# Attention with a mixture of experts on one core: where the third value product of each group stands, and where the group's output is read

## The chip, the core and the metric

The kernel runs on one core of a Trainium2 chip. Its time is device microseconds for one execution. A core has TensorE (PE in the rows, its weight loads PEld), VectorE (DVE), ScalarE (ACT), GpSimd (POOL) and SyncE (SP), which issues most of the DMAs. Each engine works through its own list of instructions in order and waits at semaphores for the others. PSUM is the memory that TensorE writes to, in banks of 2 KiB per partition.

## The reference

Attention over 4 batches of 8 heads (576 positions, 64 columns), where scores more than `tau` below their row's maximum are dropped, then a mixture of 8 experts with one expert for each token, then a dense pair of layers. The case is about the attention part alone:

```python
scores = scale * np.matmul(q, k.transpose(0, 1, 3, 2))
thresh = np.max(scores, axis=-1, keepdims=True) - tau
scores = np.where(scores >= thresh, scores, -1000000000.0)
scores = scores - np.max(scores, axis=-1, keepdims=True)
attn = np.exp(scores)
attn = attn / (np.sum(attn, axis=-1, keepdims=True) + 1e-09)
return np.matmul(attn, v).astype(np.float32)
```

## The kernel before

Attention runs as 16 units. A unit is one head of two batches, 2 times 576 rows, cut into nine tiles of 128 rows; tile 4 holds the last 64 rows of both batches. Tile `t` of unit `u` is step 9u + t, so there are 144 steps, and units are counted from 0. `Attn.run` (L325) writes the order out by hand. In step `i` every engine's list gets: the jobs of phase 0; the scores of step i + 2 (`scores`, L198, TensorE); the jobs of phase 1; row maximum and exponential of step i + 1 (`smax` L221 on VectorE, `sexp` L227 on ScalarE); mask and row sum of step i (`smask`, L240, VectorE); the threshold of step i + 1 (L231, VectorE); then the jobs of phases 2 and 3. A score tile has one of three PSUM buffers from its scores to its mask.

The jobs come from the table `PL` (L305): `"po0": (14, 2)` says that a unit's first read of outputs goes to 14 steps after the unit's first step, phase 2. `PFIRST` and `PLAST` replace entries for the first and the last unit. Within a phase, jobs stand in the order of the units.

After the mask, `split_e` (L248, ScalarE) casts a tile to 16 bits and `split_l` (L252 and L253, GpSimd) takes the remainder. When three tiles, a group, are there, `tr_e` (L259) has a DMA transpose it, issued by SP. SP also issues the swap of the halves of the queries (L195), the loads of queries, keys and values (L90 to L105), and the stores of the attention output (L300, L301). `e16`, the transpose's source, has three buffers, and `et`, its result, four.

The value products (`pv`, L282, TensorE) follow 11 steps after the tile: 14 matmuls for a tile, 28 for tile 4, each with its weights load. They write the tile `ops`, one half of it for one group and the other half for the next. `ops` shares its PSUM bank with two smaller things: the logits of the router (`lm`, which `lg_add`, L545 or L543, reads on VectorE) and a sum over the values (`vsum`, read at L132). `pv_out` (L288, VectorE; jobs `po0`, `po1`, `po2`) reads a group's half, multiplies by the reciprocals and writes `x`.

Other jobs in the places that follow: the transposes of a later unit's queries and keys on TensorE (`tr`, L164, into the one tile `tps`; the jobs `q0` and `k5` are those that the change meets) and their evacuation on ScalarE (L186, L190); the largest absolute value of the values (L123), the row sums' reciprocals (L267, L268) and the scaling of the values (L137), all on VectorE; `lg_tr` (L528) and `lg_mm` (L536) of the router on TensorE.

In steps counted from a unit's first one, its products stand at 11 to 19, always in phase 3, so the third, sixth and ninth at 13, 16 and 19. The reads stand at 14 (phase 2) and, two of them together, at 20 (phase 3), just ahead of the next unit's first product.

Of the kernel before, what the change touches and what calls it, by code (L numbers as in the profile page):

```python
# [30 lines left out]
class Attn:  # L31
# [259 lines left out]
    def store(self, u):  # L291
        nc = self.nc
        P, h = divmod(u, H)
        if h % 2 == 1:
            c = slice((h - 1) * D, (h + 1) * D)
            X = self.X[u // 2]
            for j in range(2):
# [7 lines left out]
    PL = {"lq": (-21, 1), "lk": (-31, 2), "lv": (-12, 1), "hi0": (-16, 2), "hi1": (-15, 3), "lo0": (-13, 1),  # L305
# [6 lines left out]

    PFIRST = {"hi0": (-20, 2), "hi1": (-18, 0), "lo0": (-18, 0), "lo1": (-18, 1), "q0": (-17, 0), "eq0": (-16, 2),
# [3 lines left out]
    PLAST = {"te": (4, 3), "po0": (14, 1), "po1": (17, 0), "po2": (20, 0), "rc": (11, 1), "t0": (14, 2),  # L317
             "v0": (16, 3), "l0": (20, 2), "t1": (19, 3), "v1": (20, 3), "l1": (21, 0), "t2": (20, 3), "v2": (21, 3),
             "l2": (21, 3), "la": (24, 3)}

    AFTER = ["lq hi0", "lk hi1", "hi0 lo0", "hi1 lo1", "lo0 q0", "lo0 q4", "lo0 m", "lo1 m", "lo1 k0", "lo1 k5", "q0 eq0",
             "eq0 m", "m em", "em q4", "q4 eq4", "eq4 k0", "k0 ek0", "ek0 k5", "k5 ek5", "eq0 swap", "em swap", "eq4 swap", "vm vn", "vn vc", "vc vw", "vw vh", "vh vl", "se sl", "sl te", "po2 st",
# [2 lines left out]
    def run(self, units, moe=None):  # L325
        nc = self.nc
        NU = len(units)
        sched = {}
        PL = self.PL
        for x in self.AFTER:  # L330
            x, y = x.split()
            assert PL[x] < PL[y] or PL[x] == PL[y] and list(PL).index(x) < list(PL).index(y), (x, y)

        def at(b, job, f, *a):
            i, ph = PL[job]
            sched.setdefault((b + i, ph), []).append((f, a))

        for n, u in enumerate(units):
            b = 9 * n
            PL = {**self.PL, **(self.PFIRST if n == 0 else self.PLAST if n == NU - 1 else {})}  # L340
            if n % 4 == 0:
                e0 = 0 if n else 1
                at(b, "lq", self.load_qk, u // 4, 0, e0, 4)
                at(b, "lk", self.load_qk, u // 4, 1, e0, 4)
                at(b, "lv", self.load_v, u // 4)
                for e in range(4):
                    at(b + e, "vm", self.v_max, u + e)
                at(b, "vn", self.v_sum, u)
                at(b, "vc", self.v_scale, u)
            for i in range(2):  # L350
                at(b, f"hi{i}", self.split_hi, u, i)
            for i in range(2):
                at(b, f"lo{i}", self.split_lo, u, i)
            for w in ("q0", "m", "q4", "k0", "k5"):
                at(b, w, self.tr, u, w)
                at(b, "e" + w, self.evac, u, w)
            if n == 0:
                at(b, "swap0", self.swap, u, 0, 256)
            at(b, "swap", self.swap, u, 256 if n == 0 else 0)
            at(b, "vw", self.v_w, u)  # L360
            at(b, "vh", self.v_hi, u)
            at(b, "vl", self.v_lo, u)
            for t in range(9):
                at(b + t, "se", self.split_e, u, t)
                if n == NU - 1:
                    at(b + t, "se", self.split_l, u, t // 3, slice(t % 3, t % 3 + 1), nc.vector if t in self.LD else nc.gpsimd)
                elif t % 3:
                    at(b + t, "sl", self.split_l, u, t // 3, slice(2 * (t % 3 - 1), t % 3 + 1), nc.gpsimd)
                if t % 3 == 2:
                    at(b + t - 2, "te", self.tr_e, u, t // 3)  # L370
                at(b + t, "pv", self.pv, u, t)
            for g in range(3):
                at(b, f"po{g}", self.pv_out, u, g)
            at(b, "rc", self.recip, u)
            at(b, "st", self.store, u)
            if moe and u % 2 == 1:
                P, j = u // H, u % H // 2
                for g in range(3):
                    at(b, f"t{g}", moe.lg_tr, P, j, g)
                    at(b, f"v{g}", moe.lg_ev, P, j, g)  # L380
                    at(b, f"l{g}", moe.lg_mm, P, j, g)
                at(b, "la", moe.lg_add, P, j)
        steps = [(u, t) for u in units for t in range(9)]
        ps, nn, ee = {}, {}, {}
        first, last = min(sched)[0], max(sched)[0]
        for i in range(first, last + 1):
            if i == 4 and moe:
                moe.consts()
            for f, a in sched.get((i, 0), []):
                f(*a)  # L390
            if 0 <= i + 2 < len(steps):
                ps[i + 2] = self.scores(*steps[i + 2])
            for f, a in sched.get((i, 1), []):
                f(*a)
            if 0 <= i + 1 < len(steps):
                nn[i + 1] = self.smax(ps[i + 1])
                ee[i + 1] = self.sexp(ps[i + 1], nn[i + 1])
            if 0 <= i < len(steps):
                self.smask(*steps[i], ps.pop(i), nn.pop(i), ee.pop(i))
            if 0 <= i + 1 < len(steps):  # L400
                self.sthr(nn[i + 1])
            for ph in (2, 3):
                for f, a in sched.get((i, ph), []):
                    f(*a)
# [911 lines left out]
```

## Time and profile before

| | us |
|---|---|
| median of three runs | 1117.97 (1114.81 to 1119.68) |
| the profiled execution | 1115.51 |
| its span, first to last instruction | 1113.7 |
| TensorE busy in the span | 954.5 (86%) |
| VectorE busy | 904.8 (81%) |
| ScalarE busy | 655.0 (59%) |
| GpSimd busy | 725.6 (65%) |
| value products (L282), TensorE | 101.3 |
| reads of the outputs (L288), VectorE | 15.4 in 48 |

The span is 1.8 us shorter than the execution's time. Attention fills about the first third of it, up to some 370 us; the change touches nothing behind that. In the timeline a row gives the start and the length of a piece, the engine, the line, the operation with what it writes and reads, how many were merged, and in brackets how long the engine had been idle before it and what ended that. The busy shares of the whole span are a mean over stages with different limits, so the rows below come from stretches of the attention stage.

### The profile page before, as it was taken

How to read it: one execution, taken by the hardware profiler on the slowest of the kernel's cores; microseconds unless marked ns; L12 is line 12 of the kernel's file. 1: busy time of each engine (PE TensorE's matmuls, PEld its weight loads, DVE VectorE, ACT ScalarE, POOL GpSimd, SP SyncE). 2: the span in 40 equal slices, each digit the busy share in tenths (PEclk: the TensorE clock that was granted, in tenths of full speed). 3: DMA queues.
4: the chain of work that ended last, by engine and by line, in shares of the span. 5: the costliest groups of instructions: out<-in, count | busy, mean ns of one | idle time of the engine just before them, and what ended most of it. 6: DMA issues, size and time to landing. Idle time of an engine off the chain costs nothing.

```text
span 1113.7 us, 20722 instructions
## 1 busy us (share of the span) xinstructions
PE 954.5 (86%) x7297; PEld 879.9 (79%) x7297; DVE 904.8 (81%) x1628; ACT 655.0 (59%) x1223; POOL 725.6 (65%) x629
## 2 busy tenths in 40 slices
PE   4587776885977477999999999799999999999997
PEld 3476666774876377989999999688999999999986
DVE  4898877976978559885979875799989989898894
ACT  5687875875977134443445546576665656656652
POOL 3886875775878045554565657587776767667673
PEclk9688886887889678999999999899999999999999
DMA  7999999999999666686777876320100101000000
GB/s 177 170 203 192 213 200 195 217 185 208 180 187 190 143 227 229 216 280 216 251 246 278 283 259 200 112 79 15 43 22 19 46 11 41 15 29 1 20 10 29
DMA packets 249768, 162.51 MB, mean 146 GB/s; under 512 B 180122, under 2 KB 222508, under 8 KB 249661
## 3 DMA queue, kind: packets, MB, share of 16 engines
q1 hardware_dynamic: 245901, 150.36, 56.4%
q0 software_dynamic: 3312, 10.49, 2.7%
q8 instruction: 59, 0.97, 0.3%
q10 hardware_dynamic: 448, 0.30, 0.1%
q14 instruction: 48, 0.39, 0.1%
HBM read 85.08 MB, written 23.60 MB: 98 GB/s over the span
## 4 chain that ended last, share of the span: by engine, by line
PE 45%; DVE 13%; issue 3%; ACT 2%; DMA 2%; POOL 0%; POOLq 0%; DVEq 0%; SPq 0%; ACTq 0%
PE h L1008 22%; PE y L1082 15%; PE y L1063 7%; DVE w L1195 2%; DVE w L1196 2%; DVE cv L1116 2%; DVE cm L1114 1%; DVE w L1193 1%; DVE w L978 1%; DVE cm L1118 1%; PE t L985 1%; DVE tm L1194 1%; DMA xr<-rows,idx 1%; DVE w L1197 1%; DVE hbuf L1044 1%
## 5 line engine op out<-in xcount | busy, mean ns | idle before, releaser
L252 POOL TENSOR_TENSOR e<-em,e 128x1024 f16<-128x1024 f32 (+1 forms) x98 | 158.1, 1613 | 83.8 <-ACT e L248 50.5
L1192 POOL TENSOR_SCALAR tm<-u 128x384 uint8<-128x384 f32 x88 | 128.6, 1462 | 57.5 <-ACT u L1188 56.9
L1008 PE MATMUL h<-xa,w 128*128 128x256 f32 (+6 forms) x864 | 141.6, 314 | 5.7 <-DVE hbuf L1044 4.7
L1063 PE MATMUL y<-hbuf,w 128*128 128x256 f32 (+6 forms) x864 | 141.3, 312 | 5.8 <-DVE yo L1066 5.6
L227 ACT ACTIVATE e<-sps,n 128x576 f32<-128x576 f32 x144 | 108.0, 750 | 52.4 <-DVE n L221 51.9
L1008 PEld LDWEIGHTS h<-xa,w 128*128 128x128 f32 x864 | 131.4, 195 | 8.0 <-DVE hbuf L1044 5.8
L1063 PEld LDWEIGHTS y<-hbuf,w 128*128 128x128 f32 x864 | 128.2, 192 | 7.5 <-DVE yo L1066 6.6
L978 POOL TENSOR_TENSOR w<-raw,w 128x1024 fp32r<-128x1024 f32 x36 | 91.4, 2538 | 63.5 <-ACT w L976 31.4
L240 DVE SCALAR_TENSOR_TENSOR em<-sps,n,e 128x576 f32<-128x576 f32 x144 | 116.5, 809 | 17.8 <-ACT e L227 14.8
L282 PE MATMUL ops<-vh,et 128*128 128x64 f16 (+1 forms) x2240 | 101.3, 205 | 34.0 <-DVE x L288 30.6
L221 DVE TENSOR_REDUCE n<-sps 128x1 f32<-128x576 f32 x144 | 107.2, 744 | 24.5 <-PE sps L213 24.4
L282 PEld LDWEIGHTS <-et 128*128 128x128 f16 (+1 forms) x2240 | 88.9, 110 | 45.2 <-issue 36.3
L1195 DVE SCALAR_TENSOR_TENSOR w<-y,w 128x384 f32<-128x384 f32 x96 | 122.4, 1275 | 0.0
L1188 ACT ACTIVATE u<-h 128x384 f32<-128x384 f32 x96 | 47.1, 491 | 127.0 <-PE h L1008 126.8
L213 PE MATMUL sps<-ka,qa 128*128 128x288 f32 x320 | 90.2, 376 | 28.4 <-DVE em L240 22.3
L248 ACT CAST e<-em 128x576 f16<-128x576 f32 x144 | 97.2, 676 | 22.2 <-DMA et<-e 21.0
L1008 PE MATMUL h<-xk,w 128*128 128x384 f32 x576 | 109.6, 338 | 0.7 <-DVE w L978 0.5
L1209 POOL TENSOR_TENSOR gl<-w,gh 128x384 fp32r<-128x384 f32 x83 | 84.7, 1021 | 38.8 <-ACT gh L1208 38.8
L1008 PEld LDWEIGHTS h<-xk,w 128*128 128x128 f32 x576 | 102.7, 189 | 5.2 <-DVE w L978 0.8
L1043 ACT ACTIVATE hbuf<-h 128x256 fp32r<-128x256 f32 (+6 forms) x72 | 31.1, 431 | 127.2 <-PE h L1008 127.1
L1082 PE MATMUL y<-w,gh 128*128 128x512 f32 x258 | 82.1, 399 | 6.9 <-DVE yo L1066 6.9
L976 ACT CAST w<-raw 128x1024 fp32r<-128x1024 f32 x72 | 75.3, 1050 | 19.3 <-DVE poff L576 14.7
(224 smaller groups left out, 2261.1 us busy)
## 6 DMA issues: line engine op xcount, KB each, us to landing
raw<-in_moe_w_dram SPq DMA_DIRECT2D x64, 512.0 KB, 5.2
qb<-qa SPq DMA_DIRECT2D x30, 304.0 KB, 4.8
cv<-in_moe_w_in_dram SPq DMA_DIRECT2D x16, 512.0 KB, 5.1
cv<-in_moe_w_out_dram SPq DMA_DIRECT2D x16, 512.0 KB, 4.9
wscr<-cm SPq DMA_DIRECT2D x32, 256.0 KB, 2.5
raw<-wscr SPq DMA_DIRECT2D x16, 512.0 KB, 4.0
xw<-yT SPq DMA_DIRECT2D x24, 192.0 KB, 2.4
vv<-in_v_dram SPq DMA_DIRECT2D x8, 512.0 KB, 5.7
```

What stands on the lines that cost most here:

```text
L221: nc.vector.tensor_reduce(out=n[:, 0:1], in_=ps[:, :, 0:288], axis=AX.XY, op=ALU.max, negate=True)
L227: nc.scalar.activation(out=e, in_=ps[:, :, 0:288], func=AF.Exp, bias=n[:, 0:1])
L240: nc.vector.scalar_tensor_tensor(out=self.em[u, g][:, i].rearrange("p (a b) -> p a b", a=2), in0=ps[:, :, 0:288], scalar=n[:, 1:2], in1=e, ...
L248: self.nc.scalar.copy(self.e16[u, g][:, i, 0:S], self.em[u, g][:, i])
L252: eng.tensor_tensor(out=e16[:, r, S + 64:], in0=em[:, r, 0:512], in1=e16[:, r, 0:512], op=ALU.subtract)
L282: nc.tensor.matmul(o[q], lhsT=et[:, base + c, q], rhs=vh[:, a, j, c if c < 5 else c - 5, :], start=(n == 0), stop=(n == len(terms) - 1))
L978: (self.nc.gpsimd if pool else self.nc.vector).tensor_tensor(out=l, in0=raw, in1=h.bitcast(F32), op=ALU.subtract)
L1008: self.nc.tensor.matmul(out, lhsT=a, rhs=b, start=(i == 0), stop=(i == len(parts) - 1))
L1063: nc.tensor.matmul(self.ys[d], lhsT=a[:, f % 2, s], rhs=b, start=(f == 0 and i == 0), stop=(f == 7 and i == 2))
L1082: nc.tensor.matmul(self.ys[m], lhsT=a[:, s], rhs=b[:, f % 2], start=(f == 0 and i == 0), stop=(f == 15 and i == 2))
L1192: nc.gpsimd.tensor_scalar(out=mk, in0=u, scalar1=RCUT * RCUT, scalar2=None, op0=ALU.is_gt)
L1195: V.scalar_tensor_tensor(out=w, in0=y, scalar=b, in1=w, op0=ALU.add, op1=ALU.mult)
```

## The change

The table's one entry for the value products becomes nine, one for each tile. A group's first two products stay in phase 3; its third (tiles 2, 5 and 8) moves to phase 1 of the same step, that is right behind the scores of step i + 2. The group's read moves to phase 0 of the step that follows, so it is VectorE's first instruction there: `po0` from 14 phase 2 to 14 phase 0, `po1` from 20 phase 3 to 17 phase 0, `po2` from 20 phase 3 to 20 phase 0. The last unit keeps its order. No instruction is added or removed.

```diff
-          "se": (1, 2), "sl": (2, 0), "te": (4, 2), "pv": (11, 3), "po0": (14, 2),
-          "po1": (20, 3), "po2": (20, 3), "rc": (13, 1), "st": (32, 3), "t0": (23, 1), "v0": (24, 1), "l0": (31, 2),
+          "se": (1, 2), "sl": (2, 0), "te": (4, 2), "po0": (14, 0),
+          "po1": (17, 0), "po2": (20, 0), "rc": (13, 1), "st": (32, 3), "t0": (23, 1), "v0": (24, 1), "l0": (31, 2),
...
+    for t in range(9):
+        PL[f"pv{t}"] = 11 + t, 1 if t % 3 == 2 else 3
...
+    PLAST.update({f"pv{t}": (11 + t, 3) for t in range(9)})
...
-                at(b + t, "pv", self.pv, u, t)
+                at(b, f"pv{t}", self.pv, u, t)
```

On VectorE, at the fourteenth step of a unit (here one where the values of a later head are being reduced, L123), the difference of the two orders is this. L221, L240 and L231 are row maximum, mask and threshold.

```order
 L137 TENSOR_SCALAR vv<-vv,sc 128x2x320
 L123 TENSOR_REDUCE pm<-vv 128x1
-L221 TENSOR_REDUCE n<-sps 128x1
-L240 SCALAR_TENSOR_TENSOR em,su<-sps,n,e 128x576
-L231 TENSOR_SCALAR n<-n,ntau 128x1
-L288 TENSOR_TENSOR x<-ops,r 128x3x64
+L288 TENSOR_TENSOR x<-ops,r 128x3x64
+L221 TENSOR_REDUCE n<-sps 128x1
+L240 SCALAR_TENSOR_TENSOR em,su<-sps,n,e 128x576
+L231 TENSOR_SCALAR n<-n,ntau 128x1
 L123 TENSOR_REDUCE pm<-vv 128x1
```

The first group's read goes from the end of the step to its front, ahead of the maximum and the mask.

On VectorE, at the fourteenth step of a unit where the router's logits are added, before:

```order
L137 TENSOR_SCALAR vv<-vv,sc 128x2x320
L221 TENSOR_REDUCE n<-sps 128x1
L240 SCALAR_TENSOR_TENSOR em,su<-sps,n,e 128x576
L231 TENSOR_SCALAR n<-n,ntau 128x1
L545 TENSOR_TENSOR L<-L,ops 128x8x9
L288 TENSOR_TENSOR x<-ops,r 128x3x64
L221 TENSOR_REDUCE n<-sps 128x1
```

The same place now (four lines were added to the file, so L545 has become L549):

```order
L137 TENSOR_SCALAR vv<-vv,sc 128x2x320
L288 TENSOR_TENSOR x<-ops,r 128x3x64
L221 TENSOR_REDUCE n<-sps 128x1
L240 SCALAR_TENSOR_TENSOR em,su<-sps,n,e 128x576
L231 TENSOR_SCALAR n<-n,ntau 128x1
L549 TENSOR_TENSOR L<-L,ops 128x8x9
L221 TENSOR_REDUCE n<-sps 128x1
```

The read has gone to the front, and the addition of the logits, which reads the same bank, still ends the step.

On TensorE, at the sixteenth step of a unit, before: scores, then the four transposes of a later unit's queries, then the first of the sixth product's 14 matmuls.

```order
L213 MATMUL sps<-ka,qa_108 128x288 x2
L213 MATMUL sps<-ka,qb_110 128x288 x2
L164 MATMUL tps<-identr,x_2576 128x128 x4
L282 LDWEIGHTS et
L282 MATMUL ops<-vh,et 128x64
```

The same place now, from the last of those 14 matmuls on, which follow the scores directly:

```order
L282 LDWEIGHTS et
L282 MATMUL ops<-vh,et 128x64
L164 MATMUL tps<-identr,x_2578 128x128 x4
L213 MATMUL sps<-ka,qa_108 128x288 x2
L213 MATMUL sps<-ka,qb_110 128x288 x2
```

The sixth product has passed the transposes, which now stand directly ahead of the next scores. At the thirteenth step the third product passes the transposes of `k5` in the same way; at the nineteenth there are none to pass.

## Rows read from the trace of the kernel before

**Rows 1.** Waits, whole span: who waited for whom, us in total, times, longest.

```profile
PE ops L282 <- DVE x L288: 30.6, 24, 3.0
...
DVE n L221 <- PE sps L213: 24.4, 29, 3.7
...
ACT e L248 <- DMA et<-e: 21.0, 9, 4.2
...
DVE pm L123 <- DMA vv<-in_v_dram: 11.4, 3, 4.9
```

**Rows 2.** Sums of a stretch: length, busy us of each engine, granted clock, DMA.

```profile
core 0: us, PE busy (x) PEld busy (x) DVE busy (x) ACT busy (x) POOL busy (x), PEclk, DMA share, GB/s
104.40:193.60 89.20, 64.53 (x831) 59.23 (x831) 71.79 (x176) 64.50 (x114) 64.21 (x61) 0.81 1.08 206
```

**Rows 3.** Timeline of SP, 104.3 to 193: first and last of 29 pieces.

```profile
104.49 4.12 SPq L259 DMA_TRANSPOSE et<-e  x1
...
180.77 11.48 SPq L259 DMA_TRANSPOSE et<-e  x2
```

**Rows 4.** Timeline of SP: pieces around its idle places.

```profile
57.57 1.34 SPq L90 DMA_DIRECT2D raw<-in_q_dram  x2
61.51 6.04 SPq L259 DMA_TRANSPOSE et<-e  x1
...
99.04 4.72 SPq L259 DMA_TRANSPOSE et<-e  x1
...
193.69 4.03 SPq L259 DMA_TRANSPOSE et<-e  x1
198.35 1.10 SPq L195 DMA_DIRECT2D qb<-qa  x2
200.20 5.96 SPq L259 DMA_TRANSPOSE et<-e  x1
...
277.98 4.13 SPq L259 DMA_TRANSPOSE et<-e  x1
284.08 4.67 SPq L259 DMA_TRANSPOSE et<-e  x1
```

**Rows 5.** Timeline of step 68, 186 to 194: from maximum to subtraction.

```profile
186.12 0.74 DVE L221 TENSOR_REDUCE n<-sps 128x1 f32<-128x576 f32 x1
186.78 0.80 DVE L240 SCALAR_TENSOR_TENSOR em<-sps,n,e 128x576 f32<-128x576 f32 x1
186.96 0.74 ACT L227 ACTIVATE e<-sps,n 128x576 f32<-128x576 f32 x1 [2.06 <-DVE n L221]
...
187.64 0.34 DVE L288 TENSOR_TENSOR x<-ops,r 128x192 f32<-128x192 f32 x1
...
188.04 0.91 PE L282 MATMUL ops<-vh,et 128*128 128x64 f16 x14 [2.19 <-DVE x L288]
...
188.39 2.14 POOL L252 TENSOR_TENSOR e<-em,e 128x1024 f16<-128x1024 f32 x1 [3.27 <-ACT e L248]
...
193.35 0.32 POOL L253 TENSOR_TENSOR e<-em,e 128x64 f16<-128x64 f32 x1
```

**Rows 6.** Timeline of steps 70 and 71, 191.5 to 195: transposes, maximum, product.

```profile
193.53 0.67 PE L164 MATMUL tps<-identr,x 128*128 128x128 f32 x4
193.77 0.76 DVE L221 TENSOR_REDUCE n<-sps 128x1 f32<-128x576 f32 x1 [1.11 <-PE sps L213]
...
194.00 0.69 PE L282 MATMUL ops<-vh,et 128*128 128x64 f16 x14
```

**Rows 7.** Timeline of step 115, 300 to 302.5: the same at full clock.

```profile
300.69 0.46 PE L164 MATMUL tps<-identr,x 128*128 128x128 f32 x4
...
300.95 0.75 DVE L221 TENSOR_REDUCE n<-sps 128x1 f32<-128x576 f32 x1
...
300.99 0.58 PE L282 MATMUL ops<-vh,et 128*128 128x64 f16 x14
```

**Rows 8.** Timeline, 207.9 to 209: logits added, then the product that waited.

```profile
208.33 0.21 DVE L545 TENSOR_TENSOR L<-L,ops 128x72 f32<-128x72 f32 x1
...
208.86 0.37 PE L282 MATMUL ops<-vh,et 128*128 128x64 f16 x4 [3.00 <-DVE x L288]
```

## The prediction, made before the changed kernel ran

> **What bounds the kernel now.** I started from the list of waits, because it holds the number that this change aims at: TensorE stood idle 30.6 us in 24 waits ahead of value products, each time for a read of the output bank on VectorE [rows 1]. The same list warns that idle TensorE time need not be lost time. What VectorE itself lost to late scores is 24.4 us, ScalarE lost 21.0 us to transposes that had not landed, and VectorE another 11.4 us to values that had not been loaded [rows 1]. The last two come from DMA, and no TensorE order changes them.
>
> Next I took the sums over one four-unit stretch, 104.4 to 193.6 us. In its 89.2 us no compute engine is full: VectorE is busy 71.8, TensorE 64.5, ScalarE and GpSimd 64 each, while TensorE's granted clock averages 0.81 [rows 2]. So something else sets the pace, and the reader should look at the queue that issues the DMAs, SP. From 104.49 its timeline runs through 29 pieces, transposes, swaps, loads and stores, to 180.77 + 11.48 = 192.25, each piece starting where the one before ended [rows 3]. That is 87.8 us of work in 87.8 us. The next transpose starts at 193.69 [rows 4].
>
> The queue is therefore what the attention stage waits on, and it only loses time at the few places where a transpose is not yet ready to be issued. The large ones are: before 61.51 (the last load ended at 57.57 + 1.34 = 58.91, so 2.60 idle), before 104.49 (after 99.04 + 4.72 = 103.76, 0.73), before 193.69 (1.44), before 198.35 (after 193.69 + 4.03, 0.63), before 200.20 (0.75) and before 284.08 (after 277.98 + 4.13, 1.97) [rows 3, 4]. A gain on TensorE or VectorE that does not move one of these places is taken back as a longer wait for a transpose. From 61 us on they add up to 0.73 + 1.44 + 0.63 + 0.75 + 1.97 = 5.5 us, which is about the most that any change of order can win there.
>
> **The reads move: a cost on the path.** A unit has nine value products; I count them from one, so that the third, sixth and ninth each end a group of three, and the fourth opens the second group. The chain that ends the idle time before 193.69 can be followed backwards. The GpSimd subtraction that completes the group ends at 193.35 + 0.32 = 193.67, and 0.02 later SP starts. GpSimd is busy without a break from 188.39, where it had waited 3.27 us for ScalarE; ScalarE's exponential at 186.96 had waited 2.06 us for VectorE's row maximum, which starts at 186.12 [rows 5]. This is step 68, where unit 6's first group is read (9 times 6, plus 14). Before, that read (0.34 us at 187.64) stands behind the maximum and the mask, off this chain. Now it is the step's first VectorE instruction, so the maximum, the exponential, the cast, the subtraction and the transpose all move 0.34 us later. It waits for nothing itself: the third product of the step before is long through, since VectorE is at a values reduction then. The queue is idle at that place, so 0.34 us is lost. The transposes at 61.51, 104.49 and 284.08 are the same group of their units (the second) behind the same step, so I charge them alike: 4 times 0.34 = 1.4 us.
>
> **The third product moves: TensorE's wait.** With the read at the step's front, the fourth product of step 68 is free at 186.12 + 0.34 = 186.46 instead of 188.04 [rows 5]. It starts 1.6 us sooner, but the scores behind it need a free buffer, hence the mask of that same step, which ends at 186.78 + 0.80 and now 0.34 later, at 187.92 [rows 5]. Before, they stood behind the product, which ended at 188.04 + 0.91 = 188.95; so they start some 0.8 to 1.0 earlier. Nobody is late at that point, and VectorE's next wait is three steps on: 1.11 us at 193.77 for scores [rows 6]. Here the other two edits act. The sixth product now stands ahead of the four transposes at 193.53, and the second group's read stands ahead of the maximum at 193.77. At the lower clock a product takes 0.91 [rows 5]; so without the earlier start the read could go at 193.53 + 0.91 = 194.44 and the maximum at 194.78, 1.0 later than now. With the scores 0.8 earlier it is still 0.2 later. This chain feeds the swap at 198.35 and the transpose at 200.20, where the queue idles 1.38 together [rows 4]. The bounds are a gain of 1.38 (all of it recovered) and a loss of 1.0 (nothing gained by the earlier start); I take 0, between them, as the 0.2 says.
>
> **At the full clock** the same edit costs VectorE a wait as well. In step 115 the transposes start at 300.69, so the product there (0.58) would end at 301.27 and the read at 301.61, where the maximum now starts at 300.95: 0.66 later, of which 0.34 is the read itself, taken away from step 20 of the unit [rows 7]. Net 0.32 per unit on VectorE. The queue is solid from 284.08 on, so this is hidden by transposes that wait in line; uncovered it is the slower rival below. The ninth product and its read (steps 19 and 20) keep their order against the transposes; the read moves only ahead of one maximum and one mask, and TensorE's first product of the next unit loses its wait. Moving the third product ahead of the second key transposes is hidden by a VectorE step that is long from the reciprocal and the value scaling. I price both at 0; without that cover each would cost at most its 0.58.
>
> **What stays.** All reads of this PSUM bank hold back the products, whichever columns they touch: the fourth product in row 188.04 writes one half of the bank and still waited 2.19 us for a read of the other half [rows 5]. The router's addition of logits (L545) reads the same bank, and in six units it still stands at the end of the step in which the fourth product waits; at 208.33 it ran in such a step, and the product at 208.86 had waited 3.00 [rows 8]. There only the read's 0.34 is saved. Nine units lose the wait altogether. The Trainium skill (PSUM — Partial Sum Buffer, section "PSUM bank collisions raise a hardware error") speaks against this change in the same way: it wants PSUM guarded by bank and quadrant, not by address. By that rule those six waits stay whatever columns are read, and the 3.00 in the row agrees; an order freed of them would cost 0 as well, since their end hides behind the queue.
>
> **Sum.** 1.4 + 0 + 0 = 1.4 us more. The profiled execution took 1115.51 us (span 1113.7): 1116.9. It lies 2.5 below the median of the three runs, 1117.97; the mean of all four is 1117.0, or 1.5 above it. I add that: **1118.4 us**.
>
> **Rivals.** *Faster: TensorE's stalls do set the pace.* For it speaks that VectorE's 24.4 us of waits for scores come in 29 pieces of 0.84 [rows 1], some right behind these stalls. If each of the nine freed units wins one such wait, 9 times 0.84 = 7.6, the time is 1117.0 - 7.6 = 1109.4. Against it speaks the solid queue. *Faster by the clock.* The granted clock averages 0.81 [rows 2], and 14 products took 0.91 after a stall of 2.19 against 0.58 where TensorE ran on [rows 5, 7]. If fewer stalls kept it at 2.4 GHz and all waits for scores went, 1117.0 - 24.4 = 1092.6. The Trainium skill (TensorE: Matmul & The Clock Gate, section "HAM oscillation — how this bites in real kernels") says that gaps in TensorE's work bring the lower clock back, which speaks for this rival. Against it: the gap in step 68 is only split in two by the product, and the longest gaps come from DMA.
>
> *Slower: the second group's read holds VectorE.* It is one mechanism: the read waits for a product behind which the maximum could have run. Price 0.32 per unit at the full clock and 1.0 - 0.34 = 0.67 at the lower one, some 0.5, times 15 units = 7.5, with the 1.4 above: 1117.0 + 8.9 = 1125.9. It decides from the point where VectorE's delay exceeds the time that finished groups lie waiting for SP. Against it: VectorE has 17 us free in rows 2's stretch. *It doesn't do what it says:* if the logits and other readers of the bank keep most waits, only the reads move, 1117.0 + 1.4 again, but with the 30.6 us of waits mostly still there.
>
> **How the numbers follow.** Forecast 0.64, not as said 0.06 (same time), faster 0.12, by the clock 0.03, slower 0.15. A measurement here can tell about 0.5%, 5.6 us, from no change. The forecast's own terms spread it from 1117.0 + 1.4 - 1.38 = 1117.0 to 1117.0 + 1.4 + 1.0 = 1119.4, all within that. Faster by over 0.5% gets the two rivals, 0.15; slower gets 0.15, less the part of it that stays under 5.6 us: 0.13; same 0.72. The range runs from just inside the first rival to the slower one: 1110 to 1126.
>
> **What would show it.** Right: TensorE's wait for reads falls from 30.6 to under 15 us, with what is left mostly behind L549 (the old L545); VectorE's waits for products rise from almost none; ScalarE's waits for transposes grow; SP's pieces stay end to end, and the stage ends within 3 us of where it did. The transpose that ended the idle time before 193.69 is about 0.3 later after its loads. Wrong: SP's pieces show new idle time of half a microsecond or more in most units (slower), or its idle places vanish and the last score mask comes 5 us earlier (faster).

## Result and profile after the change

The changed kernel took **1122.46 us** (median of 5 runs, 1119.30 to 1124.58) against 1117.50 (median of 5, 1114.81 to 1119.68): a ratio of **1.0055, 95% interval 1.0037 to 1.0073**, or 6.1 us slower (4.1 to 8.2). That lies inside the range of 1110 to 1126, but past the forecast of 1118.4, and its middle is just past the 0.5% that the prediction gave as what a measurement tells from no change. The profiled execution of the changed kernel took 1122.46 us, its span 1120.6.

In the changed kernel L545 has become L549 and the first copy of the logits L547. The waits that answer [rows 1], as line waited for, us in total, times, longest:

```profile
PE sps L213 <- DVE em L240: 36.7, 31, 7.4
DVE x L288 <- PE ops L282: 30.5, 18, 4.9
...
ACT e L248 <- DMA et<-e: 12.0, 5, 3.2
...
DVE n L221 <- PE sps L213: 9.3, 11, 3.6
...
PE ops L282 <- DVE L L549: 9.0, 4, 3.0
...
PE ops L282 <- DVE x L288: 6.2, 7, 2.1
...
PE ops L282 <- DVE L L547: 6.0, 2, 3.0
```

Two more waits of the kernel before:

```profile
PE sps L213 <- DVE em L240: 22.3, 13, 5.4
...
DVE x L288 <- PE ops L282: 10.6, 5, 5.1
```

The change does what it says. TensorE's waits for reads fall from 30.6 us in 24 pieces to 6.2 in 7, and six waits for the logits remain, 9.0 + 6.0 us. But TensorE now waits 36.7 us for masks, where that was 22.3: with reads, logits and masks taken together it is 57.9 us after 52.9, so its waits have moved and not shrunk. The other side shows as plainly: VectorE now waits 30.5 us in 18 pieces for products at the reads, and only 9.3 us for scores, where that was 24.4 [rows 1]. Of the waits at the reads, 10.2 us before and 9.6 now lie at the end of the last unit, which keeps its order; in the other units they grow from 0.4 to 20.9 us.

The lost time is found by cutting the attention stage in two where unit 12 begins, at its first score mask; the second piece ends with the last mask. The sums of the two stretches (length, busy us of each engine, granted clock), first of the kernel before:

```profile
core 0: us, PE busy (x) PEld busy (x) DVE busy (x) ACT busy (x) POOL busy (x), PEclk, DMA share, GB/s
62.90:286.50 223.60, 164.90 (x2100) 150.98 (x2099) 182.87 (x446) 162.99 (x287) 160.96 (x151) 0.82 1.08 200
286.50:358.50 72.00, 58.31 (x858) 53.14 (x854) 64.25 (x170) 58.98 (x101) 59.67 (x61) 0.95 1.14 188
```

And of the changed kernel:

```profile
62.80:286.20 223.40, 172.16 (x2101) 153.00 (x2100) 187.87 (x446) 162.53 (x285) 160.39 (x150) 0.82 1.08 200
286.20:365.40 79.20, 64.13 (x823) 57.11 (x823) 69.33 (x170) 58.84 (x102) 60.44 (x62) 0.85 0.92 171
```

The DVE column tells most of it. VectorE is busy 5.0 us longer in the first stretch (187.87 against 182.87) and 5.1 longer in the second (69.33 against 64.25). The first stretch takes no longer for it; the second takes 7.2 us longer. The other 2.1 us there are VectorE's own idle time.

**Where VectorE's 5 us come from** is not the reads, which take 0.35 us each as before. Two groups of instructions grew, with the same work in them. Over the whole span (line, engine, operation, count: shortest, median and longest in ns), before:

```profile
L267 DVE TENSOR_SCALAR su<-su,sc x16: 224/1126/1659, 48.9 to 358.6; 128x9 f32<-128x9 f32 x16
L137 DVE TENSOR_SCALAR vv<-vv,sc x16: 544/898/1824, 39.8 to 350.4; 128x640 f32<-128x640 f32 x16
```

After:

```profile
L267 DVE TENSOR_SCALAR su<-su,sc x16: 304/1428/1885, 48.5 to 367.1; 128x9 f32<-128x9 f32 x16
L137 DVE TENSOR_SCALAR vv<-vv,sc x16: 543/1678/1831, 39.6 to 356.7; 128x640 f32<-128x640 f32 x16
```

L267 adds a constant to a unit's nine row sums and scales them; 0.22 us is enough for it, as its shortest call shows, and 1.4 is its usual time now. In the timeline of the changed kernel one sees why:

```profile
110.77 2.16 POOL L252 TENSOR_TENSOR e<-em,e 128x1024 f16<-128x1024 f32 x1 [1.73 <-issue]
...
111.14 1.82 DVE L267 TENSOR_SCALAR su<-su,sc 128x9 f32<-128x9 f32 x1
```

L267 ends at 112.96, 0.03 behind the end of GpSimd's subtraction at 112.93. So it does in all 16 calls of the changed kernel, and before in all but one: there L267 had begun 0.1 us ahead of GpSimd and took 0.22. It is held until GpSimd's instruction is through, and the profile calls that busy. The Trainium skill (SBUF — State Buffer, section "Who interferes with whom") says that VectorE and GpSimd share one pair of SBUF ports, which a `tensor_scalar` like these two can need, and that whichever instruction issues first has it for its whole length; the trace agrees, with 0.03 us between the ends.

Behind the start of unit 12 L267 and L137 take 5.9 + 4.7 us in 4 + 4 calls, before 3.4 + 2.2: 5.0 us more, which is VectorE's added busy time there.

The reads cost VectorE idle time. Step 17 of unit 12 on VectorE in the changed kernel, with what TensorE did for it one step before and the subtraction that completes the next group on GpSimd:

```profile
303.04 0.85 PE L213 MATMUL sps<-ka,qa 128*128 128x288 f32 x2
...
303.69 0.68 PE L213 MATMUL sps<-ka,qb 128*128 128x288 f32 x2
304.17 0.97 PE L282 MATMUL ops<-vh,et 128*128 128x64 f16 x14
304.95 0.73 PE L164 MATMUL tps<-identr,x 128*128 128x128 f32 x4
305.07 0.31 POOL L253 TENSOR_TENSOR e<-em,e 128x64 f16<-128x64 f32 x1
305.18 0.36 DVE L288 TENSOR_TENSOR x<-ops,r 128x192 f32<-128x192 f32 x1 [1.86 <-PE ops L282]
305.45 0.75 DVE L221 TENSOR_REDUCE n<-sps 128x1 f32<-128x576 f32 x1
```

The scores are through at 304.37. The maximum that wants them starts at 305.45, since the read ahead of it waits for the sixth product, which at the lower clock (0.50 granted from 303 to 305.2) takes 0.97. That is 1.1 us late, the rival's 1.0 at the lower clock. In the second stretch such reads wait 7.3 us in all. Against that, VectorE's waits for scores fall from 3.8 to 1.2 us there, and one of 3.2 for an exponential is gone; with small ones, 2.1 are left.

SP's timeline shows new idle places (start, length, piece):

```profile
302.65 0.62 SPq L301 DMA_DIRECT2D rows<-x  x1
305.41 4.05 SPq L259 DMA_TRANSPOSE et<-e  x1
309.84 1.14 SPq L195 DMA_DIRECT2D qb<-qa  x2
311.68 18.32 SPq L259 DMA_TRANSPOSE et<-e  x3
330.68 1.10 SPq L195 DMA_DIRECT2D qb<-qa  x2
332.52 10.28 SPq L259 DMA_TRANSPOSE et<-e  x2
...
344.92 0.62 SPq L301 DMA_DIRECT2D rows<-x  x1
346.33 27.03 SPq L259 DMA_TRANSPOSE et<-e  x5
```

Idle before 305.41: 2.14 us; before 309.84 0.38; before 311.68 0.70; and the piece of 18.32 us for three transposes hides another 4.39. Together SP is idle 18.5 us between unit 12's first mask and the last, where it was 3.6 before. Part of this is given back: the twelve transposes themselves take 54.2 us instead of 61.6.

**How long a finished group lies waiting for SP** can be read from the same trace: from the end of the subtraction that completes it (L253) to the start of its transpose. In the changed kernel the group above is complete at 305.07 + 0.31 = 305.38 and SP takes it at 305.41, at once. The same group before:

```profile
303.65 0.30 POOL L253 TENSOR_TENSOR e<-em,e 128x64 f16<-128x64 f32 x1
...
304.66 4.86 SPq L259 DMA_TRANSPOSE et<-e  x1
```

It had waited 0.71 us. Of the twelve groups of this stretch, the kernel before left one without any wait for SP, five waited 0.2 to 0.7 us and six 1.5 to 5.9, 1.6 on average. In the changed kernel nine are taken at once, and the average is 0.2. In the first stretch the averages are 4.5 and 4.2. So the cover was thin behind the start of unit 12 to begin with, and there the changed kernel uses it up. From the transpose of 284.08 (now 283.69) to the last one SP takes 78.3 us before and 85.0 now, 6.6 more: nearly the whole difference of the two spans, 6.9.

### The profile page after: what moved, and what is told of

It reads as the page before. It is cut to its first block, busy times and chain, and to the rows that moved or that the text cites. A ratio compares the mean times of both kernels' runs of the same rounds, so it can differ in the third digit from the quotient of the medians.

```text
span 1120.6 us, 20731 instructions
## 1 busy us (share of the span) xinstructions
PE 969.5 (87%) x7297; PEld 886.7 (79%) x7297; DVE 916.4 (82%) x1628; ACT 654.2 (58%) x1223; POOL 725.2 (65%) x629
## 4 chain that ended last, share of the span: by engine, by line
PE 44%; DVE 13%; issue 3%; DMA 2%; ACT 2%; POOL 0%; POOLq 0%; DVEq 0%; SPq 0%; ACTq 0%
PE h L1012 22%; PE y L1086 15%; PE y L1067 7%; DVE w L1199 2%; DVE w L1200 2%; DVE cv L1120 2%; DVE w L982 1%; DVE cm L1118 1%; DVE w L1197 1%; DVE cm L1122 1%; DVE tm L1198 1%; DMA xr<-rows,idx 1%; PE t L989 1%; ACT w L980 1%; DVE w L1201 1%
## 5 line engine op out<-in xcount | busy, mean ns | idle before, releaser
L213 PE MATMUL sps<-ka,qa 128*128 128x288 f32 x320 | 93.8, 389 | 43.4 <-DVE em L240 36.7
L282 PE MATMUL ops<-vh,et 128*128 128x64 f16 (+1 forms) x2240 | 106.0, 210 | 22.4 <-DVE L L549 9.0
L282 PEld LDWEIGHTS <-et 128*128 128x128 f16 (+1 forms) x2240 | 91.3, 114 | 36.8 <-issue 25.0
L240 DVE SCALAR_TENSOR_TENSOR em<-sps,n,e 128x576 f32<-128x576 f32 x144 | 116.3, 807 | 3.7 <-ACT e L227 3.1
L221 DVE TENSOR_REDUCE n<-sps 128x1 f32<-128x576 f32 x144 | 106.8, 742 | 9.7 <-PE sps L213 9.3
L213 PEld LDWEIGHTS sps<-ka,qa 128*128 128x128 f32 x320 | 57.4, 226 | 52.6 <-DVE em L240 25.2
```

Of the source, the lines that this page charges most:

```text
L213: nc.tensor.matmul(ps[:, c, 0:288], lhsT=w[:, o:o + 128], rhs=ka[:, j, 288 * c:288 * c + 288], start=(i == 0), stop=(i == n - 1))
L221: nc.vector.tensor_reduce(out=n[:, 0:1], in_=ps[:, :, 0:288], axis=AX.XY, op=ALU.max, negate=True)
L240: nc.vector.scalar_tensor_tensor(out=self.em[u, g][:, i].rearrange("p (a b) -> p a b", a=2), in0=ps[:, :, 0:288], scalar=n[:, 1:2], in1=e, ...
L282: nc.tensor.matmul(o[q], lhsT=et[:, base + c, q], rhs=vh[:, a, j, c if c < 5 else c - 5, :], start=(n == 0), stop=(n == len(terms) - 1))
```

## Experiments

Three theories stood at the start. **A:** the second group's read, held by the sixth product, delays VectorE. **B:** VectorE meets GpSimd at other moments and is held longer. **C:** the first read ahead of the maximum, my forecast's only term, is the loss. Each kernel below was timed beside the kernel before on the same chip (medians 1116.48, 1115.87 and 1117.34 us in the three groups); a ratio of 1.001 is 1.1 us.

### The three groups apart

In the schedule table a job has a step of the unit and a phase. Each kernel moves the products of one or two groups and their reads:

```
 kernel before: "pv": (11, 3) for all nine, "po0": (14, 2), "po1": (20, 3), "po2": (20, 3)
 first alone:   third product  phase 1, "po0": (14, 0)
 second alone:  sixth product  phase 1, "po1": (17, 0)
 third alone:   ninth product  phase 1, "po2": (20, 0)
 second undone: third and ninth product phase 1, "po0": (14, 0), "po2": (20, 0)
```

> Only the third product of each unit is moved behind its scores, and only the first group's read (po0) stands first in step 14; the other two groups are as before the change. Theory A (the loss comes from the second group's read, which waits for the sixth product): close to the kernel before, between 0.5 us faster and 1.4 us slower, and the last score mask within 1.5 us of 358.5. Theory B (the loss comes from VectorE's operations meeting GpSimd's at other moments, above all the nine-column row-sum operation L267): part of the 5 us whichever part of the change is made, so 1.5 to 3 us slower, with L267's sum above 18 us (15.2 before, 23.1 after). Theory C (the first read at the step's front, my term of the prediction, is the loss): 4 to 6 us slower.

> Only the sixth product is moved behind its scores, and only the second group's read (po1) stands first in step 17. Theory A: nearly the whole loss, 4 to 6 us slower than before, with VectorE's waits at po1 for the sixth product of 1 us or more in units 12 to 14, and the last score mask 4 to 7 us later than 358.5. Theory B: 1.5 to 3 us slower, and the size goes with L267's sum and not with the waits at po1. Theory C: within 1.5 us of before.

> Only the ninth product is moved behind its scores, and only the third group's read (po2) stands first in step 20; the second group is read at step 20 behind its exponential, as before. Theories A and C: within 1 us of before. Theory B: 0 to 3 us slower, going with L267's sum.

> The changed kernel with the second group's part undone: the sixth product again behind the transposes of its step, its read again at step 20 behind the exponential; the third and the ninth product and their reads as in the changed kernel. Theory A: the loss is gone, 0 to 1.5 us slower than before, about 4 us faster than the changed kernel, and SP's new idle places between 300 and 365 us are gone. Theory B: 2 to 4 us slower than before, unless L267's sum falls back to 15 us. Theory C: 4 to 6 us slower.

Measured: first alone 1117.72 us, ratio 1.0014 (1.0001 to 1.0028), 1.6 us; second alone 1121.86, 1.0050 (1.0036 to 1.0064), 5.6 us; third alone 1116.55, 1.0004 (0.9991 to 1.0017), 0.4 us; second undone 1119.47, 1.0027 (1.0013 to 1.0041), 3.0 us. C falls. The second group carries most, as A says, and more than B alone allowed for; but without it half of the loss stays, which is B's figure and twice A's most. The parts alone add up to 7.6 us against 6.1 for the whole, which their intervals do not tell apart. L267 and L137 together take 36.4, 40.4, 36.3 and 41.0 us in these four kernels, 33.2 before and 43.5 in the changed kernel: where more is held, more is lost, in broad terms. The second piece of the stage in the kernel with the second group undone:

```profile
288.50:362.30 73.80, 60.49 (x851) 54.68 (x850) 67.05 (x171) 58.85 (x101) 59.68 (x61) 0.91 1.08 184
```

It takes 73.8 us with VectorE busy 67.05, between the 72.0 and 79.2 above; a finished group waits 0.8 us for SP on average there, between 1.6 and 0.2. But VectorE's busy time alone does not set the length: with the first and with the third group alone it is busy 66.6 us in this stretch, 2.3 to 2.4 more than before, and the stretch takes 72.3 and 72.0, with the groups waiting 2.1 and 1.9 us on average. The profiled execution of the kernel with the second group alone (1116.80 us) was the quickest of its six and so says little on its median.

### What VectorE's time costs, early and late

Work of known length, and nothing else, was added to the kernel before, at the place of the second read. These reductions take 0.80 to 0.81 us each, all twenty of the early dose.

```
+    def dose(self):
+        for i in range(2):
+            self.nc.vector.tensor_reduce(out=self.dz[:, i:i + 1],
+                in_=self.c14.unsqueeze(1).to_broadcast([128, 5, 128]), axis=AX.XY, op=ALU.max)
...
+            if u in range(2, 12):        # late: range(12, 15)
+                sched.setdefault((b + 17, 0), []).append((self.dose, ()))
```

> The kernel before, with nothing moved, and 1.4 to 1.5 us of added VectorE work (two reductions of 128x640 constants, by the 0.81 us of the 128x640 reductions and the 0.74 of the scores' ones) as the first thing of step 17 of units 2 to 11, before the row maximum: 14 to 16 us of VectorE work in all, at the place where the second group's read waits in the changed kernel. If SP's queue takes up what VectorE loses until about 284 us (my forecast's reason, and why the changed kernel's transposes run level with the old ones up to there): 0 to 2 us slower, and the transposes after 284 start within 2 us of the kernel before. If it does not: 7 to 15 us slower.

> The same two added reductions at the front of step 17, but only in units 12 to 14, 4.3 to 4.9 us of VectorE work in all. If what VectorE loses there is no longer covered, because SP has no more loads to issue for later units: 2.5 to 5 us slower, with new idle time on SP between 300 and 365 us, as in the changed kernel. If the solid queue covers it there too, as the prediction said: under 1 us slower, and the changed kernel's loss must come from something else than VectorE's wait at the second read.

Measured: early, 15.3 us of work cost 2.5 us (1119.43, ratio 1.0022, 1.0009 to 1.0036). Late, 4.6 us cost 3.7 (1119.73, ratio 1.0033, 1.0018 to 1.0048). The two stretches, early dose:

```profile
62.70:287.00 224.30, 164.96 (x2105) 150.03 (x2104) 195.65 (x465) 163.57 (x286) 160.55 (x150) 0.83 1.09 199
287.00:359.00 72.00, 58.28 (x848) 53.79 (x847) 67.34 (x173) 59.54 (x103) 59.88 (x61) 0.93 1.11 188
```

Late dose:

```profile
63.30:287.30 224.00, 164.49 (x2104) 150.38 (x2102) 182.63 (x446) 162.19 (x284) 160.25 (x150) 0.82 1.09 198
287.30:361.80 74.50, 57.53 (x850) 52.34 (x849) 70.84 (x176) 59.22 (x103) 60.79 (x62) 0.95 1.12 187
```

With 12.8 us more on VectorE the first stretch is 0.7 us longer. With 6.6 us more (two thirds of it the dose) the second is 2.5 longer, and the timed cost is four fifths of the dose. By the timed medians, then, a microsecond of VectorE costs a sixth of itself up to unit 12 and four fifths behind it; the intervals of the two rates, 0.07 to 0.26 and 0.4 to 1.2, do not overlap. Where the late dose's 3.7 us are lost the trace does not show. It left SP idle for 4.2 us behind the start of unit 12, against 3.6 before, so one expectation failed; finished groups still waited 2.5 us for SP on average, SP took the same 78.3 us to its last transpose, and 1.7 of the 4.4 us between the two profiled spans stand ahead of the first dose, where the kernels are the same. In the early dose's kernel VectorE is busy 3.1 us more in the second stretch too, half of it two of the added reductions, and that stretch takes 72.0 us as before. New idle time on SP comes with the whole loss, not with every delay of VectorE.

### The row sums' scaling in another form

```
-        nc.vector.tensor_scalar(out=su, in0=su, scalar1=1e-9, scalar2=self.vs[u][1], op0=ALU.add, op1=ALU.mult)
+        nc.vector.scalar_tensor_tensor(out=su, in0=su, scalar=1e-9, in1=self.vs[u][1].to_broadcast([128, 9]),
+                                       op0=ALU.add, op1=ALU.mult)
```

> The changed kernel, with the nine-column row-sum operation (L267) written as a scalar-tensor-tensor operation whose second operand is the scale broadcast over the nine columns; the numbers computed are the same. In the changed kernel L267 takes 23.1 us in 16 calls, between 0.28 and some 1.8 each, against 15.2 before. Theory B (VectorE's operations of this form meeting GpSimd's are the loss): L267's sum falls under 6 us and the time by 3 to 6 us, to the time of the kernel before or below. Theory A (the second group's read): 0 to 2 us faster than the changed kernel, still 4 us or more behind the kernel before.

> The kernel before with the same rewriting of L267, nothing else. It shows what the operation's long form costs without the change: theory B says it gains clearly less than the changed kernel does, 0 to 2 us; theory A says both gain alike, within 1.5 us of each other. If the rewritten form takes as long as the old one, both are within 0.5 us of their own kernels.

Measured: in the changed kernel 1118.55 us, ratio to the kernel before 1.0013 (0.9996 to 1.0029); in the kernel before 1114.43, ratio 0.9983 (0.9967 to 0.9999). L267 in the changed kernel with the new form:

```profile
L267 DVE SCALAR_TENSOR_TENSOR su<-su,sc x16: 157/1421/1925, 48.0 to 359.2; 128x9 f32<-128x9 f32 x16
```

Its median is 1.421 us against 1.428. The rewriting freed it in four of 16 calls only (0.16 us each), so it does not test B as it was meant to. Both kernels gained, by 4.7 us and 1.9 us. In the changed kernel L267 and L137 together fell from 43.5 to 38.8 us, behind the start of unit 12 from 10.6 to 8.0, where L137 alone fell, which the rewriting does not touch; this goes the way B says (in a profiled execution 3.5 us quicker than the median), but whether it makes up the gain is not shown. The Trainium skill's section named above could have told so: it also counts VectorE instructions with two inputs in SBUF among those that meet a GpSimd instruction that reads SBUF. The longest call, 1.9 us, agrees.

### The scaling off VectorE

```
-        nc.vector.tensor_scalar(out=su, in0=su, scalar1=1e-9, scalar2=self.vs[u][1], op0=ALU.add, op1=ALU.mult)
         nc.vector.reciprocal(out=r, in_=su)
+    def rscale(self, u):
+        su = self.sums[u]
+        self.nc.scalar.activation(out=su, in_=su, func=AF.Copy, scale=self.vs[u][1])
...
+            sched.setdefault((b + 12 if n < NU - 1 else b + 10, 2), []).append((self.rscale, (u,)))
```

> The kernel before, with the nine row sums of a unit scaled on ScalarE at step 12 of the unit (the added 1e-9 is dropped, which a sum of at least 1 does not feel in fp32); VectorE is left with the reciprocal. In every trace so far L267 on VectorE ends 0.02 to 0.03 us behind the end of a GpSimd subtraction, whenever that began first, in either form of the operation, so the rewriting did not take the wait away. Without L267 on VectorE its 15.2 us there go, 3.4 of them behind the start of unit 12, where VectorE is idle only 7.7 of 72.0 us: 1 to 4 us faster than before, by both theories. If the place where it is held only moves to the values scaling (L137), under 1 us.

> The changed kernel with the same scaling on ScalarE. L267 takes 23.1 us there, 5.9 behind the start of unit 12, 2.5 more than before. Theory A alone (the second read's wait is the loss): the changed kernel stays 4 to 6.5 us behind the kernel before with the same scaling. Theory B as a part: the distance between the two shrinks by about 2.5 us, to 3 to 4. Theory B alone: it shrinks to under 1.5 us.

Measured: in the kernel before 1115.57 us, ratio 0.9988 (0.9971 to 1.0005); in the changed kernel 1116.61, ratio 0.9989 (0.9972 to 1.0007). **The distance between the two is gone**: their means of 12 runs each differ by 0.2 us, plus or minus 1.5. This is what B alone forecast, and A alone is out. (The changed kernel with its old scaling was not timed again in this group; its 6.1 us are from the first one.) The reads still wait in the changed kernel, though. Its second stretch, and VectorE's waits in it:

```profile
282.80:355.30 72.50, 59.95 (x811) 53.42 (x811) 62.43 (x166) 59.65 (x106) 60.58 (x62) 0.88 1.07 188
```

```profile
DVE x L291 <- PE ops L285: 4.2, 3, 1.9
...
DVE r L267 <- ACT su L272: 1.8, 4, 0.9
DVE n L221 <- PE sps L213: 0.9, 2, 0.6
```

The stretch takes 72.5 us, as before the change (72.0, and 73.5 in the kernel before with the same scaling), with 4.2 us of waits at the reads and with a granted clock of 0.88, near the changed kernel's 0.85. So neither the waits at the reads nor the clock suffices for the loss. VectorE is busy 62.43 us instead of 69.33, and a finished group waits 1.5 us for SP on average, where it was 0.2 in the changed kernel. The kernel before gained little from the same edit because its reciprocal (now L267) waits 14.9 us in 13 pieces for ScalarE, as long as the held operation took; in the changed kernel it waits 9.7 us where L267 took 23.1. I read this as one account: without the held operations VectorE has room for the waits at the reads, and with them it has not. The groups' waits for SP agree, but that any other relief of VectorE of this size would not have done the same was not tested.

### The reads behind the mask

```
 reads late, second group: sixth product phase 1, "po1": (17, 2); the rest as in the kernel before
 reads late, all groups:   all three products phase 1, "po0": (14, 2), "po1": (17, 2), "po2": (20, 2), scaling on ScalarE
```

> Only the sixth product is moved behind its scores, as in the run with the second group alone; its read stands at step 17 behind the maximum and the mask, no longer ahead of them. Theory A (the read holds back the maximum): the loss of the run with the second group alone, 5.4 us, goes: 0 to 1.5 us slower than before, and VectorE waits less than 3 us for products at the read in units 2 to 14 (14.5 us in the run with the read first). If it is TensorE's new order, the product ahead of the transposes, that costs: 3 to 6 us slower still.

> The changed kernel's three early products, with every read of a group at the same step as in the changed kernel but behind the maximum and the mask, and with the row sums scaled on ScalarE. If VectorE's order is what counts and TensorE's is not: level within 1.5 us with the kernel before with that scaling, 1 to 4 us faster than the kernel before. If TensorE's earlier products are worth something once VectorE is not held by them: faster than that by 2 us or more. If the early products cost in themselves: slower than the kernel before.

Measured: the second group 1118.46 us, ratio 1.0027 (1.0006 to 1.0047); all groups with the scaling on ScalarE 1115.56, ratio 0.9988 (0.9968 to 1.0009). The waits at the read are gone in the first, but 3.0 us of loss are left in its median, with so wide a spread (1114.56 to 1124.40) that neither 1.5 nor 5 is excluded: this run is inconclusive. The second is level with the kernel before that has the same scaling (difference of the means 0.1, plus or minus 1.8). TensorE's earlier products are worth nothing that these runs show, within some 2 us, even where VectorE is not held by them. None of the versions beats the kernel before by 0.5%.

## Why the prediction was partly right

**SP sets the pace and takes back what the engines gain or lose:** right up to unit 12. The transpose of [rows 4] at 284.08 starts at 283.69 in the changed kernel, the one at 193.69 at 192.15, and 15.3 us of added work cost 2.5.

**The first read costs 1.4 us:** the first group alone cost 1.6 (0.1 to 3.1). The size agrees, within a wide interval and perhaps by luck. That it is lost at the four idle places is not shown: three of those four transposes start earlier in the changed kernel than before.

**The third group at 0:** 0.4 us alone, right.

**The sixth product and the second read at 0:** this is the step that failed. The prediction worked out a delay of 0.32 us at full clock and 1.0 at the lower one, and then set it to nothing, since "the queue is solid from 284.08 on, so this is hidden by transposes that wait in line". Alone this group costs 5.6 us. A queue whose pieces touch is not a queue with much work waiting: behind 284.08 half of the groups had lain finished for 0.7 us or less when SP took them, so delays of 0.3 to 1.1 us could not hide behind that for long, and in the changed kernel nine of twelve were taken at once. VectorE had little room to catch up, busy 64.25 of 72.0 us behind unit 12's start; a sum over that stretch, as was made for 104.4 to 193.6, would have shown it. The prediction also took the full clock there from one step [rows 7]; it fell from 0.95 to 0.85.

**What was missing from the sum:** the operations that GpSimd holds. VectorE's two held groups grew from 33.2 to 43.5 us, 5.0 of it behind unit 12's start. Both stood in the trace as busy VectorE, L267 at 0.95 us on average for nine columns, and the prediction took busy time for work.

**The slower rival** named the read's wait and the condition, that VectorE's delay exceeds what finished groups wait for SP. Its place was right, its spread over 15 units was not: the cost falls in the last units, and with L267 off VectorE it did not show at all.

**The faster rivals** fall: TensorE's waits for reads fell by 24 us and nothing came of it; the clock went down, not up. **What stays** was right in kind: six logit waits were forecast, 4 + 2 are there. Of the signs to look for, TensorE's waits for reads and logits came to 21.2 us, not under 15; VectorE's waits for products rose as said, though they started from 10.6 us and not from almost none, nearly all of it in the last unit; ScalarE's waits for transposes fell from 21.0 to 12.0, where I had them grow; the last score mask came 6.9 us later, not within 3.

**What stays open:** how the 6.1 us divide between the reads' waits and the held operations. L137 was not taken off VectorE. Why the other form of L267 gained is not known, nor where the late dose was paid.

## To carry to other kernels

A queue whose pieces touch covers a delay only as long as finished work lies waiting for it: read that time, group by group. Cut a stage where the queue runs out of other work (here behind the last load for a later unit, issued at 263.85 in the kernel before), and ask for the bound of each piece: a delay that cost a sixth of itself in the first cost four fifths in the second, by the timed doses. Look for instructions whose longest time is many times their shortest; their busy time can be a wait for another engine, and reordering changes it. An early product only moves the wait if the engine that reads it has something else to do first.

## What the hardware showed

A VectorE scaling on nine columns takes 0.22 us when GpSimd leaves it alone (0.16 in the two-operand form) and up to 1.89 when it begins behind a GpSimd subtraction (1.93 in the two-operand form), and then ends 0.02 to 0.03 us behind it. The 128x640 scaling L137 goes from 0.54 to 1.83. Next to them the 128x9 reciprocal (0.215 to 0.218), which reads what L267 writes, the 128x1 threshold (0.20 to 0.215) and the 128x640 reductions (0.80 to 0.82) never stretch in the changed kernel, though 11 of 16, 92 of 144 and 2 of 16 of them begin while a GpSimd instruction runs. The opposite order is seen too; before, where VectorE began first:

```profile
245.69 0.55 DVE L137 TENSOR_SCALAR vv<-vv,sc 128x640 f32<-128x640 f32 x1
245.83 1.68 POOL L119 TENSOR_TENSOR x<-raw,x 128x576 fp32r<-128x576 f32 x1
```

L137 keeps its 0.55, and GpSimd's operation takes 1.68 instead of the 1.40 to 1.45 that it takes where L137 comes second. With less than 0.1 us between the two starts, the profile does not tell which one will be held: in the changed kernel L137 starts 0.04 to 0.05 us ahead of that operation in nine calls, and is held in six of them, while GpSimd's takes 1.76 to 1.77 in the other three.
